# The tail of a one-token decode block: the folded sum kept in PSUM, two engines copying it out, and a store of four 512-byte rows

## The chip, the core and the metric

The kernel runs on one core of one Trainium2 chip. The core has five engines with their own instruction streams (TensorE or PE for matrix products, VectorE or DVE, ScalarE or ACT, GpSimd or POOL, SyncE or SP for issuing transfers), which meet only through semaphores, and 16 DMA engines that move data between HBM and the on-chip memory SBUF. TensorE writes its products to a second on-chip memory, PSUM (128 partitions, 8 banks of 512 fp32 numbers on each). The metric is the device time of one execution in microseconds; lower is better.

## The reference, cut to what matters

One token `x` of width 1024 goes through two branches, and the results are added to it.

```python
xn = layernorm(x)
# A: attention of 32 heads over the last W = 4096 places of a cache with 4 key/value heads
q = (xn @ wq)                                  # 1024 -> 32 heads x 128
p = softmax(q . k_cache[:, :, Sk - W:, :] * 128 ** -0.5)
A = (p . v_cache[:, :, Sk - W:, :]).reshape(4096) @ wo      # 4096 -> 1024
# B: a second layernorm and an MLP
B = gelu(layernorm(xn) @ w1 + b1) @ w2 + b2    # 1024 -> 3584 -> 1024
return x + A + B
```

Every weight and cache entry is used once. In bf16 wq, wo, the keys' window and the values' window and w1 and w2 come to some 39.9 MB that must be read from HBM; the output is 1024 bf16 numbers, 2 KB.

## The kernel before, in words

All big loads are issued by SP on one queue, in this order: wq in two pieces, the key window, w1, the value window; w2 once the product with wq is done (it takes over wq's place in SBUF); wo once the product with w1 is done (it takes over the places of w1 and of the keys). wo is laid out so that each of the 128 partitions holds 32 consecutive rows of it; "row j" below is the j-th row of every partition, a 128 x 1024 slab. Its 32 rows come in pieces of 16, 8, 4 and 3 rows (`WO_CHUNKS`), and row 31 comes as two loads, one for each half of its 1024 columns, with a semaphore each (lines 425 to 427).

TensorE multiplies a vector by such slabs with the array cut into four column groups of 32: a column of the vector, repeated 32 times, is the stationary operand, and the slab streams past. Four rows are worked on at a time, one in each group, so that partitions 0, 32, 64 and 96 of two PSUM banks (`SB` and `SB + 1`, banks 4 and 5, half the columns each) collect four partial sums. Both w2's 28 rows (`row_loop`) and wo's rows 0 to 27 (`four_rows`) add to them, and so do x and b2: lines 541 to 543 multiply a selection matrix `SELX` by `XB4`, which holds x's quarters on partitions 0, 32, 64, 96 and b2's on 1, 33, 65, 97.

Around the pieces of wo PE waits for transfers. After each of the first three pieces the kernel issues one fp32 product of no use (`keep_busy`, line 298; 512, 320 and 128 columns by `BUSY`), whose result nobody reads.

What follows row 27 is the tail:

- the copies: DVE copies bank 4 and ACT bank 5 to SBUF as `S` (lines 554 and 555)
- the fold: four fp32 matmuls of 256 columns (line 559) multiply a vector with ones at partitions 0, 32, 64, 96 by `S`. Column group a gets the a-th 128 columns of either half, into bank 0
- rows 28 to 31 (`fin_load`, `fin_half`): here all four column groups work on the same row, each on its own 128 columns of one half, so that nothing is left to be folded. The halves go to banks 7 and 6 (`HB`). Rows 28 to 30 wait for the piece of three rows; the first half of row 31 waits for its load, the second half for its own
- the end: DVE copies the fold from bank 0 to SBUF (`BULK`, line 578); then for each half it adds `BULK` and the bank into `ORow` as bf16 (line 582); SP waits for the second addition and issues the store of `ORow` (line 585), as eight runs of 256 bytes, two from each of four partitions; and SP waits for that store to land.

The small loop written behind the last matmul (lines 571 to 574) is a branch that PE takes once; the change doesn't touch it.

## Time and profile before

| | |
|---|---|
| three runs | 99.14, 99.17 and 99.19 us, median 99.17 |
| the profiled execution | 99.34 us, of which the span from the first to the last instruction is 98.0 |
| busy in the span | PE 53.2 us, PE's weight loads 13.4, DVE 41.8, ACT 11.2, POOL 8.2 |
| read from HBM | 39.86 MB, 407 GB/s over the span |
| queue of SP and ACT | 1740 packets, 95.0% of the 16 DMA engines' span |
| mean granted TensorE clock | 0.93 of full speed |
| the store's issue on SP (line 585) | 0.69 us, from 96.27 |

The times in the profile are microseconds from the first instruction of the span. A row of the timeline gives the start, the length, the engine and line, the operation with what it writes and reads, and how many instructions it merges; in square brackets is how long the engine had been idle and what released it. PEld stands for PE's weight loads, SPq and ACTq for the queues of DMA issues. A table by stretches gives for each stretch of time its length, then the busy time of each engine with the number of instructions, the granted PE clock, the share of the DMA engines and their rate.

### The profile page before, as it was taken

The numbers are of one execution on the slowest core, as the hardware profiler recorded it, in microseconds if no ns is written. First come the engines' busy times: TensorE is split into PE (matmuls) and PEld (weight loads), VectorE is DVE, ScalarE is ACT, GpSimd is POOL, SyncE is SP. The second block draws the span as 40 slices with busy tenths as digits, with TensorE's granted clock in tenths as the row PEclk, the third lists the DMA queues.
The fourth block names the chain that finished last, engine by engine and source line by source line (L and its number), as shares of the span: only waits on it lengthen the run. The fifth ranks groups of instructions, "written<-read, shape, count | busy, mean of one in ns | idle before, by whom it ended". The sixth has DMA issues, their size and how long they took to land.

```text
span 98.0 us, 911 instructions
## 1 busy us (share of the span) xinstructions
PE 53.2 (54%) x376; PEld 13.4 (14%) x217; DVE 41.8 (43%) x45; ACT 11.2 (11%) x21; POOL 8.2 (8%) x33
## 2 busy tenths in 40 slices
PE   0000232007960947195361489878998677883781
PEld 0000220001100001011010111113332111220130
DVE  0000321000028899999999500987943400110042
ACT  0000527000022000000000489000000000000020
POOL 6776201000000000000000000000000000000000
PEclk9999999999999589957999755899999999999999
DMA  3999888999999988899599998889994999999960
GB/s 53 488 613 398 377 374 375 398 538 441 428 428 578 398 374 374 374 398 702 237 428 428 428 588 374 374 374 398 702 398 214 428 428 428 421 428 408 421 251 1
DMA packets 1765, 39.87 MB, mean 407 GB/s; under 512 B 216, under 2 KB 484, under 8 KB 612
## 3 DMA queue, kind: packets, MB, share of 16 engines
q1 hardware_dynamic: 1740, 39.85, 95.0%
q10 hardware_dynamic: 24, 0.01, 0.0%
q14 instruction: 1, 0.01, 0.0%
HBM read 39.86 MB, written 0.00 MB: 407 GB/s over the span
## 4 chain that ended last, share of the span: by engine, by line
DMA 52%; DVE 24%; PE 11%; POOL 5%; issue 3%; SPq 1%; ACT 1%; POOLq 0%; DVEq 0%
DMA KT<-in_A_k_cache_dram 26%; DMA KT<-in_A_wo_dram 26%; DVE KT L355 18%; PE PS L292 9%; DVE MX L375 2%; DVE MX L377 2%; POOL F L206 1%; POOL B1R L188 1%; SPq L166 1%; DVE KT L554 1%; DVE MR L388 1%; PE PS L559 1%; ACT Q L381 1%; POOL QB L198 1%; PE PS L283 1%
## 5 line engine op out<-in xcount | busy, mean ns | idle before, releaser
L355 DVE STREAM_TRANSPOSE KT<-KT 128x4096 bf16<-128x4096 bf16 x4 | 17.4, 4413 | 0.5 <-DMA KT<-in_A_k_cache_dram 0.5
L283 PE MATMUL PS<-KT,QB 128*128 128x512 bf16 x32 | 8.9, 427 | 7.6 <-DVE KT L355 7.6
L283 PE MATMUL PS<-WA,XNTb 128*32 128x512 bf16 x64 | 6.8, 605 | 7.4 <-DMA WA<-in_A_wq_dram 7.4
L292 PE MATMUL PS<-W,YTb 128*32 x64 | 8.2, 464 | 1.3 <-issue 0.9
L292 PE MATMUL PS<-V,WA 128*128 (+1 forms) x31 | 7.9, 381 | 0.5 <-issue 0.2
L292 PE MATMUL PS<-WA,GT 128*32 x56 | 6.7, 381 | 2.6 <-issue 1.8
L253 PE MATMUL PS<-XT,onesf 128*128 128x16 f32 x2 | 0.6, 385 | 10.9 <-POOL XT L251 10.9
L327 DVE CAST Q<-PS 128x512 bf16<-128x512 f32 x1 | 0.7, 691 | 12.6 <-PE PS L283 12.6
L242 DVE STREAM_TRANSPOSE XT<-XB 128x256 bf16<-128x256 bf16 x1 | 0.6, 625 | 9.7 <-DMA XB<-in_A_x_dram 9.7
L406 DVE STREAM_TRANSPOSE WA<-WA 128x4096 bf16<-128x4096 bf16 x1 | 4.4, 4436 | 0.0
L292 PE MATMUL PS<-W,OT 128*32 128x512 bf16 x48 | 2.9, 380 | 2.1 <-DMA W<-in_A_wo_dram 1.5
L367 PEld LDWEIGHTS <-QB 128*128 128x128 bf16 x16 | 1.7, 104 | 17.3 <-DVE KT L355 13.5
L554 DVE COPY KT<-PS 128x512 f32<-128x512 f32 x1 | 0.7, 692 | 7.6 <-PE PS L292 7.6
L520 DVE TENSOR_TENSOR OD<-PS,D 128x128 f32<-128x128 f32 x1 | 0.3, 292 | 8.4 <-PE PS L518 8.4
L292 PEld LDWEIGHTS PS<-V,WA 128*128 (+1 forms) x32 | 3.1, 96 | 4.7 <-issue 3.0
L283 PE MATMUL PS<-MRow,ML 128*128 128x512 bf16 x8 | 3.3, 581 | 0.7 <-DVE QB L348 0.7
L402 ACT ACTIVATE WA<-PS,NMB 128x1024 bf16<-128x1024 f32 (+1 forms) x2 | 3.1, 1536 | 1.2 <-DVE NMB L397 1.2
L381 ACT ACTIVATE Q<-PS 128x512 f32<-128x512 f32 x1 | 0.6, 597 | 22.5 <-DVE MX L377 22.5
L555 ACT ACTIVATE KT<-PS 128x512 f32<-128x512 f32 x1 | 0.6, 597 | 22.2 <-PE PS L292 22.2
L312 PEld LDWEIGHTS <-XNTb 128*32 128x32 bf16 x32 | 1.2, 138 | 12.1 <-DMA WA<-in_A_wq_dram 8.3
L292 PEld LDWEIGHTS PS<-W,YTb 128*32 x32 | 1.6, 98 | 7.5 <-issue 7.1
L257 ACT ACT_TABLE_LOAD x1 | 1.3, 1283 | 10.9 <-POOL XT L251 10.9
(105 smaller groups left out, 47.4 us busy)
## 6 DMA issues: line engine op xcount, KB each, us to landing
WA<-in_A_wq_dram SPq DMA_DIRECT2D x1, 7168.0 KB, 21.5
W<-in_B_w_dram SPq DMA_DIRECT2D x1, 7168.0 KB, 42.2
WA<-in_B_w_dram SPq DMA_DIRECT2D x1, 7168.0 KB, 47.4
KT<-in_A_k_cache_dram SPq DMA_DIRECT2D x1, 4096.0 KB, 25.9
V<-in_A_v_cache_dram SPq DMA_DIRECT2D x1, 4096.0 KB, 51.3
W<-in_A_wo_dram SPq DMA_DIRECT2D x1, 4096.0 KB, 18.9
W<-in_A_wo_dram SPq DMA_DIRECT2D x1, 2048.0 KB, 23.4
WA<-in_A_wq_dram SPq DMA_DIRECT2D x1, 1024.0 KB, 5.0
```

Of the source, the lines that this page charges most:

```text
L257: C["std1"] = ACT.mark(act.activation(out=msx[:, 6:7], in_=msx[:, 5:6], func=ACTF.Sqrt, scale=-1.0, bias=EPSC[:, 0:1]))
L283: return pe.add_instruction(mybir.InstMatmult(name=nc.get_next_instruction_name(), engine=PEE, ldweights=load, start_tensor_calc=start, st ...
L292: return pe.add_instruction(mybir.InstMatmult(name=nc.get_next_instruction_name(), engine=PEE, ldweights=load, start_tensor_calc=start, st ...
L312: pe.ldweights(w, tile_position=(0, 32 * a))
L355: C["kt"].append(d(dve.transpose(KT[:, j * W:(j + 1) * W], KT[:, j * W:(j + 1) * W])))
L367: pe.ldweights(w, tile_position=(0, 0))
L375: d(dve.tensor_reduce(out=MX[:, 0:1], in_=PS[:, 0:2048], axis=AX.X, op=ALU.max))
L377: C["mx1"] = d(dve.tensor_reduce(out=MX[:, 1:2], in_=PS[:, 2048:4096], axis=AX.X, op=ALU.max))
L381: C["s7"] = ACT.mark(act.activation(out=S7, in_=bank(7), func=ACTF.Copy))
L402: C[f"exp{j}"] = C["exp"] = ACT.mark(act.activation(out=PT[:, lo:lo + n], in_=src, func=ACTF.Exp, bias=NMB[:, 0:1], scale=SCALE, accum_out ...
L406: C["PT"] = d(dve.transpose(PT, PT))
L554: C["S0"] = d(dve.tensor_copy(S[:, 0:DH2], bank(SB)))
```

## The change

- x and b2: one weight load of all of `SELX` and two matmuls of 128 columns on the whole array, which start banks 7 and 6 anew. They no longer go into banks 4 and 5.
- The fold is eight fp32 matmuls of 128 columns that add to banks 7 and 6 in place of four of 256 columns that start bank 0. Column group a now holds the a-th quarter of the output, its first 128 columns in bank 7 and the others in bank 6.
- Rows 28 to 31 add to the same places, and none of them starts a bank.
- The third `keep_busy` (128 columns, after row 27) is gone.
- Row 31 is one load with one semaphore, and both of its halves wait for that.
- The copy `BULK` and the two additions are gone: ACT copies bank 7 and DVE bank 6 into `ORow`, and SP waits for both. The store has four runs of 512 bytes.

```diff
-BUSY = (512, 320, 128)
+BUSY = (512, 320)
...
-    out_rows = out.rearrange("b s (h a n) -> (b s a) h n", h=2, a=4)
+    out_rows = out.rearrange("b s (a n) -> (b s a) n", a=4)
...
-    for h in range(2):
-        sp.dma_start(KT[:, 7 * D + h * DH2:7 * D + (h + 1) * DH2], wo_p[:, 31, h * DH2:(h + 1) * DH2]).then_inc(
-            s_wo[4 + h], 16)
+    sp.dma_start(KT[:, 7 * D:8 * D], wo_p[:, 31, :]).then_inc(s_wo[4], 16)
...
-    def fin_half(c, h, first, last):
+    def fin_half(c, h):
         for a in range(4):
-            lo = (c - WO_W1) * D + h * DH2 + a * DQ
-            ins = held(PS[32 * a:32 * a + 32, HB[h] * 512:HB[h] * 512 + DQ], KT[:, lo:lo + DQ],
-                       OT[:, c:c + 1].to_broadcast([128, 32]), (0, 32 * a), (128, 32), first, last)
+            lo = (c - WO_W1) * D + a * 2 * DQ + h * DQ
+            ins = go(quarter(a, h), low(KT[:, lo:lo + DQ], OT[:, c:c + 1].to_broadcast([128, 32])), (0, 32 * a), (128, 32),
+                     False, True, True, False)
         return ins
+    def quarter(a, h):
+        return PS[32 * a:32 * a + 32, HB[h] * 512:HB[h] * 512 + DQ]
...
-    for a in range(4):
-        pe.matmul(bank(SB + a // 2, (a % 2) * 256, 256)[32 * a:32 * a + 32, :], lhsT=SELX[:, 32 * a:32 * a + 32],
-                  rhs=XB4[:, :], start=False, stop=True, skip_group_check=True)
+    pe.ldweights(SELX[:, :], tile_position=(0, 0))
+    for h in range(2):
+        go(bank(HB[h], 0, DQ), low(XB4[:, h * DQ:(h + 1) * DQ], SELX[:, :]), (0, 0), (128, 128), True, True, True, False)
...
-        keep_busy(BUSY[j])
+        else:
+            keep_busy(BUSY[j])
...
-    for a in range(4):
-        last = pe.matmul(PS[32 * a:32 * a + 32, 0:2 * DQ], lhsT=I32[:, 0:1].to_broadcast([128, 32]),
-                         rhs=S[:, :].rearrange("p (h y) -> p h y", h=2)[:, :, a * DQ:(a + 1) * DQ], start=True, stop=True)
-    C["bulk"] = PE.mark(last)
+    for h in range(2):
+        for a in range(4):
+            pe.matmul(quarter(a, h), lhsT=I32[:, 0:1].to_broadcast([128, 32]),
+                      rhs=S[:, a * 2 * DQ + h * DQ:a * 2 * DQ + (h + 1) * DQ], start=False, stop=True, skip_group_check=True)
...
     fin_load(31)
+    pe.wait_ge(s_wo[4], 16)
     for h in range(2):
-        pe.wait_ge(s_wo[4 + h], 16)
-        C[f"fin{h}"] = PE.mark(fin_half(31, h, False, True))
+        C[f"fin{h}"] = PE.mark(fin_half(31, h))
...
-    dve.wait_ge(PE.sem, C["bulk"])
-    d(dve.tensor_copy(BULK[:, :], bank(0, 0, 2 * DQ)))
-    dw()
-    for h in range(2):
-        dve.wait_ge(PE.sem, C[f"fin{h}"])
-        C["out"] = d(dve.tensor_tensor(out=ORow[:, h * DQ:(h + 1) * DQ], in0=bank(HB[h], 0, DQ),
-                                       in1=BULK[:, h * DQ:(h + 1) * DQ], op=ALU.add))
-    sp.wait_ge(DVE.sem, C["out"])
-    sp.dma_start(out_rows, ORow[0:128:32, :].rearrange("p (h n) -> p h n", h=2)).then_inc(s_out, 16)
+    act.wait_ge(PE.sem, C["fin0"])
+    C["out0"] = ACT.mark(act.activation(out=ORow[:, 0:DQ], in_=bank(HB[0], 0, DQ), func=ACTF.Copy))
+    dve.wait_ge(PE.sem, C["fin1"])
+    C["out1"] = d(dve.tensor_copy(ORow[:, DQ:2 * DQ], bank(HB[1], 0, DQ)))
+    sp.wait_ge(ACT.sem, C["out0"])
+    sp.wait_ge(DVE.sem, C["out1"])
+    sp.dma_start(out_rows, ORow[0:128:32, :]).then_inc(s_out, 16)
     sp.wait_ge(s_out, 16)
```

More of the change, by code (lines that the diff above doesn't have):

```diff
@@ L80, in bass_parallel_sum__sliding_block_cached__mixer_channel_mlp__decode_kernel @@
     s_v = sems("s_v", 1)
-    s_wo = sems("s_wo", len(WO_CHUNKS) + 2)
+    s_wo = sems("s_wo", len(WO_CHUNKS) + 1)
     s_w2 = sems("s_w2", len(W2_CHUNKS))
@@ L142, in bass_parallel_sum__sliding_block_cached__mixer_channel_mlp__decode_kernel @@
     OT = sb("OT", [128, 32], bf16)
-    BULK = sb("BULK", [128, 256], f32)
     ZERO = sb("ZERO", [128, 1], bf16)
@@ L565, in bass_parallel_sum__sliding_block_cached__mixer_channel_mlp__decode_kernel @@
         for h in range(2):
-            fin_half(c, h, c == WO_BULK, False)
+            fin_half(c, h)
     fin_load(31)
+    pe.wait_ge(s_wo[4], 16)
     for h in range(2):
-        pe.wait_ge(s_wo[4 + h], 16)
-        C[f"fin{h}"] = PE.mark(fin_half(31, h, False, True))
+        C[f"fin{h}"] = PE.mark(fin_half(31, h))
     nc.br("once", engines=[PEE])
```

## The prediction

> **What bounds the kernel now.** I read the page first. Its slices of DMA use are at 8 or 9 nearly everywhere up to the third from the last; the kernel streams 39.86 MB at 407 GB/s over the span, and the last bytes of wo come at the end.

> ```profile
> DMA  3999888999999988899599998889994999999960
> ```

> Nothing in the change touches the stream before wo's last row, so I next read the chain of waits from there, cut to the tail, to see what is left after the last byte.

> ```profile
> 67.64 25.42 DMA KT<-in_A_wo_dram
> ...
> 94.51 0.64 PE PS L559 x8
> 95.15 0.50 PE PS L283 x28
> ...
> 95.75 0.50 DVE ORow L582 x2
> ```

> The chain goes through the copy (0.70, left out here) and the fold (line 559). Whether they really decide is seen from row 31's matmuls. Here is the table by stretches for line 283 alone (length, PE busy, number of instructions):

> ```profile
> 95.40:95.60 0.20, 0.20 (x20) 1.00 0.16 41
> 95.60:95.64 0.04, 0.03 (x4) 1.00 0.00 0
> 95.64:95.68 0.04, 0.00 (x0) 1.00 0.00 0
> 95.68:95.92 0.24, 0.22 (x4) 1.00 0.00 0
> ```

> All but four of the 32 matmuls of rows 28 to 31 are over at 95.64, then PE is empty, and the last four run alone from 95.69. So the end is set by the landing of row 31's second half, and copy and fold have time to spare. The transfers agree: the last packets in the stretch from 95.0 (40 slices of 10 ns) are those of one late DMA engine, one line of 1 KB every 42 ns.

> ```profile
> GB/s 0 102 0 0 0 102 0 0 0 0 102 0 0 0 102 0 0 0 0 0 0 0 0 0 0 0 0 0 0 0 0 0 0 0 0 0 0 0 0 0
> ```

> After that, the timeline and, for the store's packets, the transfers from 97.4 (40 slices of 10 ns again):

> ```profile
> 95.41 0.50 PE L283 MATMUL PS<-KT,OT 128*32 128x128 bf16 x8
> 95.75 0.50 DVE L582 TENSOR_TENSOR ORow<-PS,BULK 128x128 bf16<-128x128 f32 x2
> 96.27 0.69 SPq L585 DMA_DIRECT2D out_dram<-ORow  x1
> ...
> GB/s 0 0 0 0 0 0 0 0 0 0 0 0 0 0 0 0 26 26 51 52 0 26 0 26 0 0 0 0 0 0 0 0 0 0 0 0 0 0 0 0
> ```

> The two additions take 0.292 us each and overlap (0.50 together), so the second starts at 95.96, on the heels of the last matmul (95.69 + 0.24 = 95.93), and ends at 96.25. SP issues at 96.27 for 0.69 (96.96), the packets start 0.61 later (97.56 to 97.65), and the span ends at 98.02. The largest piece of this tail is the store: 1.75 us, of which 0.69 is its issue.

> **The change part by part**, against the profiled execution: 98.0 of span and 1.3 around it make 99.34, which is 0.17 above the median of 99.17. Differences are carried over to the median.

> 1. Row 31 as one load. A late engine has 8 lines of 2 KB to move in place of 16 of 1 KB. At the stream's 428 GB/s (26.8 per engine, the page's slices for wo) 1 KB would take 38 ns; it takes 42, so a line costs 4 ns of its own. Eight lines fewer are 0.035, the completion write of the other load about 0.01: landing 0.045 earlier. Ends: 0 (the lines overlap anyway) and 0.07 (twice the 4 ns). SP issues one load less (0.45 us, line 426), at 69 us, when nothing waits for SP.

> 2. Both halves of row 31 wait for it. Formerly the first half's four matmuls ran in the shadow of the second half's landing; now eight follow the landing. 20 matmuls in 0.20 us after 95.40 were mostly tails; the pace is that of 24 matmuls of rows 28 to 30 from 95.07 to 95.41, 0.34 us for six groups of four: 0.056 a group. So +0.055, and the last result is at 95.69 - 0.045 + 0.055 + 0.24 = 95.94.

> 3. The copies. `BULK`'s copy (0.42) lay beside the matmuls and its removal gives nothing. DVE's copy of 128 columns: copies of 512 and 256 columns took 0.692 and 0.425, so 128 take 0.292, as the addition did: 0. ACT's copy of bank 7 is not in the trace; the nearest row is 32x128 in 0.27 (line 350). It begins 0.055 before DVE's and is no longer, so it ends first: 0. If it cost as much as ACT's 512 columns (0.60) it would end 0.25 after DVE; that is an upper end I don't take, since 512 columns are four times the work.

> 4. SP waits twice. The wait for ACT is one more instruction, over before DVE's copy ends if ACT is first; the chain's row for such an instruction on DVE (line 581) is 0.02. I take +0.02; ends 0 and 0.05.

> 5. The store's issue, the term that matters. SP's rows for one-level patterns after an idle time (line 166: wq, w2, wo's first) are 0.383, 0.336 and 0.328; its only row for a two-level pattern after an idle time is the key window's, 0.642, and the store before is two-level too, at 0.687. After the change it is one-level, four lines.

> ```profile
> L173 SPq DMA_DIRECT2D KT<-in_A_k_cache_dram x1: 642/642/642, 6.4 to 6.4; - x1
> ...
> L166 SPq DMA_DIRECT2D W<-in_A_wo_dram x2: 328/380/433, 66.8 to 67.2; - x2
> ...
> L246 ACTq DMA_DIRECT2D XB<-in_B_b_dram x1: 503/503/503, 10.3 to 10.3; - x1
> ```

> The row of the same shape, four lines of 512 B, is ACT's load of b2: 0.503. So the gain is 0.18 by that row and 0.26 to 0.31 by SP's own (0.642 less 0.383 or 0.328). The queue that issues is SP, so I take its smallest, -0.26, with b2's 0.18 pulling the same way. Ends: 0 (it is the only store in the trace, and the length may be the store's own) and -0.36 (0.687 less 0.328). A loss is out: only the kernel's first load on ACT was longer than 0.687, and that was the first of its queue.

> 6. The store's data. The eight packets of 256 B, two on each of four engines, lie within 0.1 us; four of 512 B carry the same bytes. I take 0; ends 0 and -0.05 (half of the 0.1).

> [...]

> 7. The fold. Sixteen instructions of 128 columns in place of eight of 256, as much to stream. The old ones start in two groups (four in 94.47:94.75, the others to 95.06), 0.24 each, and all eight weight loads are over in the first. Expected 4 x 0.12, the same 0.48. Bounds: 0.48, and +0.42 if each of the four groups waits for a weight load of 0.106. Cover: rows 28 to 30 need 0.34 and row 31 can't start before 95.645, so the fold may last until 95.30, 0.31 later than now. At 0.42 it costs 0.11; I take 0.

> 8. x and b2. Four weight loads and four matmuls (0.29 us from 85.33) become one and two. PE waits for `OT` until 86.18 either way: 0.

> 9. The third `keep_busy` (0.49 us from 93.65) ran in the wait for DVE's copy, until 94.47: 0 if the clock holds.

> Sum: -0.045 + 0.055 + 0.02 - 0.26 = -0.23: 99.34 becomes 99.11, the median 98.94.

> **Rivals.**

> *The store's issue keeps its length.* Then -0.045 + 0.055 + 0.02 = +0.03: 99.20, no change. For it: no other store is in the trace. Against it: SP's one-level and two-level rows differ. At b2's 0.503 the sum is -0.15, 99.02, and that, too, counts as the same.

> *The 256-byte writes were slow to finish*, and wider ones aren't. The span ends 0.37 us after the store's last packet; that is the most that can go, and with half of it gone the sum is -0.23 - 0.18: 98.76. Against it: from the last packet of row 31 (95.19) to the matmul that waited for it (95.69) are 0.50, so small writes finish no later than large loads.

> *The clock falls without the third `keep_busy`* (slower). The table by stretches of 3.4 us, the length of the clock's steps here (length, PE busy, PE loads, DVE, ACT, POOL, clock, DMA):

> ```profile
> 38.27:41.69 3.42, 0.99 (x6) 0.19 (x2) 3.42 (x2) 0.00 (x0) 0.00 (x0) 1.00 0.66 285
> 41.69:45.10 3.41, 2.69 (x7) 0.30 (x2) 3.41 (x1) 0.00 (x0) 0.00 (x0) 0.50 1.24 538
> ...
> 89.47:92.89 3.42, 1.77 (x18) 0.50 (x10) 0.00 (x0) 0.00 (x0) 0.00 (x0) 1.00 0.99 412
> ...
> 91.60:95.01 3.41, 2.33 (x24) 0.85 (x16) 0.69 (x1) 0.60 (x1) 0.00 (x0) 1.00 0.92 364
> ```

> After the stretch with 0.99 us busy the next runs at 0.50; after the one with 1.77 the clock stays at 1.00. The stretch with the third `keep_busy` would go from 2.33 to 1.84, above 1.77. Should it fall all the same, fold (0.48), rows 28 to 30 (0.34) and row 31 (0.11) double; less the 0.31 of cover that is +0.62, with the store's gain +0.39: 99.55. [...]

> *The fold overruns* (slower): if all 16 weight loads of 0.106 stand in line with the matmuls it lasts 1.7 us longer, 1.4 beyond the cover: 100.3. Against the old 0.48 it is slower from 1.22 us on (0.48, 0.31 of cover, the 0.23 of gain, and 0.2). The eight loads of the old fold stood in nobody's way.

> **How the numbers follow.** Forecast, with the issue between 0.33 and 0.48 us: 52 in 100, -0.16 to -0.35, 98.82 to 99.00, nearly all of it faster. Issue longer than that: 24, from 99.0 to 99.22, the same. Slow small writes on top: 6, 98.6 to 98.8, faster. Clock: 5, 99.55. Fold or a wait behind it (ACT's copy at its upper end, +0.25): 13, 99.4 to 100.3, slower, less 1 that ends at the same. About 0.2% (0.2 us) is what a measurement here tells from no change. Moving some 7 of the forecast's 52 that give less than 0.2 us to the same: faster 0.51, same 0.30, slower 0.19. The range reaches from 98.75 to 99.40: it leaves out half of the slow small writes and most of the slower cases. The likeliest case's own is 98.82 to 99.00.

> **What would show it.** The issue on SP at 0.33 to 0.5 us in place of 0.69; eight matmuls of row 31 in one run of some 0.28 us behind one landing near 95.64; ACT's copy over before DVE's; SP's issue within 0.05 of 96.28; the sixteen fold instructions over by 95.3; the clock at 1.00 to the end. I am wrong if the issue stays near 0.69, if row 31's first matmul comes later than 95.7 because rows 28 to 30 are late, or if the clock shows 0.5 in the tail.

## The result

| | kernel before | changed kernel |
|---|---|---|
| median, 22 executions each | 99.19 us (99.09 to 99.49) | 99.83 us (99.10 to 100.27) |
| ratio | 1 | 1.0051, 95% interval 1.0031 to 1.0072 |
| the profiled execution | 99.34 us, span 98.0 | 100.17 us, span 97.9 |
| span, all executions of the changed kernel | | 97.8 to 98.1 us |
| total less span | 1.3 us in the profiled one | 1.27 to 1.36 us in ten executions, 1.92 to 2.37 us in twelve |

The change makes the kernel slower, where 98.94 was forecast, and the median lies outside the range (98.75 to 99.40). The last row of the table is needed to understand the number: the executions of the changed kernel fall into two groups, which have the same span and differ only in the time around it. Below, an execution with 1.6 us or more around its span is called one with a *late end*. Without the late ends the median of the changed kernel is 99.26, 0.07 above the kernel before.

There are then two results to explain: inside the span nothing was gained, where 0.23 us had been forecast, and outside it 0.6 to 1.1 us were lost in about half of the executions.

### The profile page after: what moved, and what is told of

It reads as the page before. It is cut to its first block, busy times and chain, and to the rows that moved or that the text cites. A ratio compares the mean times of both kernels' runs of the same rounds, so it can differ in the third digit from the quotient of the medians.

```text
span 97.9 us, 916 instructions
## 1 busy us (share of the span) xinstructions
PE 52.5 (54%) x380; PEld 13.1 (13%) x220; DVE 41.2 (42%) x43; ACT 11.4 (12%) x22; POOL 8.2 (8%) x33
## 3 DMA queue, kind: packets, MB, share of 16 engines
HBM read 39.86 MB, written 0.00 MB: 407 GB/s over the span
## 4 chain that ended last, share of the span: by engine, by line
DMA 54%; DVE 24%; PE 10%; POOL 5%; issue 3%; SPq 2%; ACT 1%; POOLq 0%
DMA KT<-in_A_wo_dram 28%; DMA KT<-in_A_k_cache_dram 26%; DVE KT L354 18%; PE PS L291 9%; DVE MX L374 2%; DVE MX L376 2%; SPq L165 2%; POOL F L205 1%; POOL B1R L187 1%; DVE MR L387 1%; ACT Q L380 1%; POOL QB L197 1%; POOL I L198 0%; POOL XB L186 0%; POOL identf L195 0%
## 6 DMA issues: line engine op xcount, KB each, us to landing
WA<-in_B_w_dram SPq DMA_DIRECT2D x1, 7168.0 KB, 47.4
```

## The profile after, inside the span

The page of the changed kernel: its span, and the use of the DMA engines in 40 slices.

```profile
span 97.9 us, 916 instructions
...
DMA  2998888999999988899699998888994999999960
```

The stream looks as before. Next, the tail from the timeline of the changed kernel (start, length, engine and line, operation, how many; in brackets the idle time before it and what ended that).

```profile
93.69 0.69 DVE L555 COPY KT<-PS 128x512 f32<-128x512 f32 x1 [7.63 <-PE PS L291]
94.44 0.38 PEld L561 LDWEIGHTS PS<-KT,I 128*32 128x32 f32 x16 [1.30 <-DVE KT L555]
94.44 0.64 PE L561 MATMUL PS<-KT,I 128*32 128x128 f32 x16 [0.79 <-DVE KT L555]
...
94.93 0.89 PE L291 MATMUL PS<-KT,OT 128*32 128x128 bf16 x32
95.81 0.28 ACT L579 ACTIVATE ORow<-PS 128x128 bf16<-128x128 f32 x1 [1.51 <-PE PS L291]
95.86 0.29 DVE L581 CAST ORow<-PS 128x128 bf16<-128x128 f32 x1 [1.48 <-PE PS L291]
96.25 0.66 SPq L584 DMA_DIRECT2D out_dram<-ORow  x1
```

Three things are to be seen. The 16 fold instructions have their weight loads behind them at 94.82 (94.44 + 0.38), and rows 28 to 30, whose piece lands at 94.89, start at 94.93: the fold does not overrun. The two copies take 0.28 and 0.29 us, and ScalarE's, which starts first, ends first (96.08 against 96.15). And the store's issue takes 0.66 us; the forecast had 0.43.

The table by stretches for the line that issues row 31's matmuls (length, PE busy and number of instructions, PE loads, clock, DMA share, GB/s):

```profile
95.50:95.54 0.04, 0.00 (x0) 0.00 (x0) 1.00 0.00 0
95.54:95.60 0.06, 0.06 (x6) 0.00 (x0) 1.00 0.00 0
95.60:95.66 0.06, 0.06 (x8) 0.00 (x0) 1.00 0.00 0
95.66:95.90 0.24, 0.16 (x8) 0.00 (x0) 1.00 0.00 0
```

PE is empty ahead of 95.54, since row 31's load lands at 95.50; then all eight matmuls of the row run behind that landing, the second half starting 0.055 us after the first. The clock is 1.00 in all of these stretches.

## The profile after, outside the span

The page ends with the span. The transfers of the changed kernel's profiled execution after it, from 98.5 to 100.6 (40 slices of 52.5 ns), are one packet:

```profile
DMA  0000000000000090000000000000000000000000
...
DMA packets 1, 0.02 MB, mean 8 GB/s; under 512 B 0, under 2 KB 0, under 8 KB 0
...
q8 instruction: 1, 0.02, 3.3%
```

It begins in the fifteenth slice, at 99.24 to 99.29, and takes 3.3% of sixteen engines' 2.1 us, which is 1.1 us of one engine. It is 16 KB that the profile calls "instruction"; I take it for a block of a program on its way into an engine. An 8 KB one on another queue (q14) is in the profile of nearly every kernel here; in this one it starts at 95.49 and takes 0.44 us, in the kernel before at 95.55 and 0.51, beside the tail. The one of 16 KB comes 1.3 us after the span's end and is over near 100.4. The profiled execution has a late end (2.27 us around the span, 100.17 in all).

Which engine's program? The packet's row doesn't say. On the page TensorE runs by far the most instructions (380 products and 220 weight loads, where VectorE has 43, GpSimd 33 and ScalarE 22), and the compiled program tells what the change did to its length: it grew from 435 to 442 instructions, 16 more for the fold, 5 fewer for x and b2, 4 fewer without the third `keep_busy`. That the block is TensorE's was thus an assumption at first; what speaks for it is `e11_before_pad12` below, where twelve weight loads more on TensorE and nothing else bring a packet of this size and queue into the stream. So the experiments began with the question whether TensorE's longer program, ScalarE's late copy, the wider rows of the store or the missing `keep_busy` made the late end.

## Experiments: which part makes the late end

In the expectations of the first runs the theories are these: the length of TensorE's program (A, where a letter stands for it), ScalarE's copy as one of the last instructions (B), the store's wider rows (C), the changed order of TensorE's last instructions (D) and the missing `keep_busy` (E).

**TensorE's program lengthened alone** (`e1_before_pad7`), the kernel before:

```diff
+    for _ in range(7):
+        pe.ldweights(ML[:, :], tile_position=(0, 0))
     pe.ldweights(ML[:, :], tile_position=(0, 0))
```

> The kernel before with seven more weight loads of the mask ML on PE (where PE waits for DVE's transposes anyway), so that PE's stream has 442 instructions as the changed kernel's has, in place of 435. In the changed kernel the span is 97.8 to 98.1 us in all 22 executions, but half of them take 1.3 us around it and half 2.0 to 2.3. Theory A (PE's stream has grown by seven instructions over a limit, and the end of the program is fetched late): some executions near 100.1, others near 99.2, spans near 98.0. Theory B (ACT now ends its program 1.8 us later) and theory C (the store's four wide rows, or SP's second wait): all executions within 99.1 to 99.5.

Measured: 99.2 us, ratio 1.0011 (1.000 to 1.0023); one execution of 11 had 1.65 us around its span, the others 1.30 to 1.35. The length 442 is not enough for what the change does.

**No ScalarE at the end** (`e2_after_dve_copies`), the changed kernel with both copies on VectorE and one wait on SyncE:

```diff
-    act.wait_ge(PE.sem, C["fin0"])
-    C["out0"] = ACT.mark(act.activation(out=ORow[:, 0:DQ], in_=bank(HB[0], 0, DQ), func=ACTF.Copy))
+    dve.wait_ge(PE.sem, C["fin0"])
+    d(dve.tensor_copy(ORow[:, 0:DQ], bank(HB[0], 0, DQ)))
...
-    sp.wait_ge(ACT.sem, C["out0"])
```

> The changed kernel with both final copies on DVE, so that ACT's last instruction is again the copy of S at 94 us, and SP waits once. PE's stream stays at 442 instructions. The span should be 0.2 longer (two copies of 0.29 that overlap a little), 98.1. Theory A: still two groups of times, 0.8 to 1.0 apart. Theory B, and SP's second wait: one group near 99.4. The store's rows: two groups.

**A late ScalarE copy in the kernel before** (`e3_before_act_late`), whose result nobody reads:

```diff
+    act.wait_ge(PE.sem, C["fin1"])
+    act.activation(out=LATE[:, :], in_=bank(SB, 0, DQ), func=ACTF.Copy)
```

> The kernel before with one copy by ACT of 128 columns of an idle bank behind the last matmul, into a scratch tile that nobody reads or waits for. PE's stream stays at 435 instructions. Theory A: one group near 99.2. Theory B: two groups, near 99.2 and 100.1.

Measured: without ScalarE at the end the changed kernel still has a late end in 4 of 12 executions (1.95 to 2.49), median 99.28, ratio 1.0044 (1.0017 to 1.0071). The kernel before with a late ScalarE copy has 99.2 us, ratio 1.0006 (0.9996 to 1.0017), and one execution of 11 at 1.64. So the late end doesn't need ScalarE at the end, and a late ScalarE copy alone doesn't bring it.

**The kernel before with one load for row 31 and a store of four 512-byte rows** (`e6_before_load_store`); the columns of fold and rows 28 to 31 are renumbered as in the change:

```diff
-    out_rows = out.rearrange("b s (h a n) -> (b s a) h n", h=2, a=4)
+    out_rows = out.rearrange("b s (a n) -> (b s a) n", a=4)
...
-        sp.dma_start(KT[:, 7 * D + h * DH2:7 * D + (h + 1) * DH2], ...
+    sp.dma_start(KT[:, 7 * D:8 * D], wo_p[:, 31, :]).then_inc(s_wo[4], 16)
...
-    sp.dma_start(out_rows, ORow[0:128:32, :].rearrange("p (h n) -> p h n", h=2)).then_inc(s_out, 16)
+    sp.dma_start(out_rows, ORow[0:128:32, :]).then_inc(s_out, 16)
```

> The kernel before with row 31 as one load and the store as four rows of 512 bytes (the columns of fold and rows 28 to 31 are mapped to suit), all else as it was: fold in bank 0, BULK, two additions, three keep_busy, 435 instructions on PE. Theory C: two groups of times, near 99.2 and 100.1. Theories D and E: one group. By the profile after, the span should be that of the kernel before within 0.1, since the store's issue took 0.66 us there, too.

Measured: 99.41 us in four executions, ratio 0.9992 (0.9936 to 1.0048; two of the seven executions of the kernel before beside it have a late end), 1.3 us around the span in all. That no late end shows in four executions says little of the rows of the store: if a third were late, four would be free of it once in five times. The issue of the store, here with one wait and with neither the new fold nor the new copies, takes 0.652 us:

```profile
L583 SPq DMA_DIRECT2D out_dram<-ORow x1: 652/652/652, 96.5 to 96.5; - x1
```

**No `keep_busy` at all** (`e4_after_no_busy`), to see whether the clock or its margin has a part:

```diff
-        else:
-            keep_busy(BUSY[j])
```

> The changed kernel without the two remaining keep_busy products, 434 instructions on PE. Theory A: one group, and if the clock holds near 99.1 (span 97.9, 1.2 to 1.3 around it). Theories B and C: still two groups. The stretches without these products have 1.0 us or less of PE work in 3.4 us, so the granted clock may fall to one half in the tail; then the rows from 94.4 on take twice as long and the span is up to 0.6 longer.

Measured: 100.19 us, ratio 1.0114 (1.0097 to 1.0131), but in the span (98.7 to 98.9); one late end in five. The table by stretches of the clock's steps, for this kernel and then for the changed one (length, busy time of PE, PE loads, DVE, ACT, POOL, clock, DMA share, GB/s):

```profile
89.01:92.42 3.41, 1.04 (x16) 0.20 (x8) 0.00 (x0) 0.00 (x0) 0.00 (x0) 1.00 0.95 398
92.42:95.83 3.41, 2.11 (x33) 0.99 (x28) 0.69 (x1) 0.60 (x1) 0.00 (x0) 0.50 0.65 263
```

```profile
92.77:96.18 3.41, 1.88 (x56) 0.85 (x36) 0.98 (x2) 0.88 (x2) 0.00 (x0) 1.00 0.58 232
89.36:92.77 3.41, 1.77 (x18) 0.50 (x10) 0.00 (x0) 0.00 (x0) 0.00 (x0) 1.00 0.95 395
```

After a stretch with 1.04 us of PE work the clock is at 0.50 and the tail longer by 1 us; after stretches with 1.77 and 1.88 it stays at 1.00. The first two `keep_busy` together are worth that microsecond, the third was not needed. The margin is small: in the last run below (`e18_after_pv3_swap`) a stretch with 1.61 us, from 93.17 to 96.58, is followed by 0.50. It costs nothing there, since TensorE's work is over, but in the stretches at the end of these traces 1.77 us of work held the clock and 1.61 didn't.

## Experiments: the length of TensorE's program

The next three undo or add single parts, and they showed something that none of the theories above had.

**The third `keep_busy` put back** (`e5_after_busy3`), 446 instructions:

```diff
-BUSY = (512, 320)
+BUSY = (512, 320, 128)
...
-        else:
-            keep_busy(BUSY[j])
+        keep_busy(BUSY[j])
```

> The changed kernel with the third keep_busy (128 columns) put back, 446 instructions on PE. Theory D (the changed order of PE's last instructions makes the end of its program late): two groups of times again, near 99.2 and 100.1, since PE's stream is no shorter. Theory E (the dropped product leaves PE cold or idle at the end, and that makes the end late): one group near 99.2. Theory C (the store's four wide rows): two groups.

**The kernel before with the fold in PSUM and two copies** (`e7_before_fold_in_psum`), 447 instructions; the third `keep_busy` is left out here, too, and rows 28 to 31 add to the fold, while x and b2, the two loads of row 31 and the two-level store stay as before:

```diff
-    for a in range(4):
-        last = pe.matmul(PS[32 * a:32 * a + 32, 0:2 * DQ], ...
+    for h in range(2):
+        for a in range(4):
+            pe.matmul(PS[32 * a:32 * a + 32, HB[h] * 512:HB[h] * 512 + DQ], lhsT=I32[:, 0:1].to_broadcast([128, 32]),
+                      rhs=S[:, h * DH2 + a * DQ:h * DH2 + (a + 1) * DQ], start=True, stop=True, skip_group_check=True)
...
+    C["out0"] = ACT.mark(act.activation(out=ORow[:, 0:DQ], in_=bank(HB[0], 0, DQ), func=ACTF.Copy))
+    C["out"] = d(dve.tensor_copy(ORow[:, DQ:2 * DQ], bank(HB[1], 0, DQ)))
```

> The kernel before with the fold as eight matmuls into banks 7 and 6, rows 28 to 31 adding to it, no third keep_busy, and the two results copied by ACT and DVE; x and b2, the two loads of row 31 and the store of eight runs stay as before. 447 instructions on PE. Theory D: two groups of times. Theory C: one group near 99.2. Theory E: two groups.

**The changed kernel with 24 weight loads more, early in the program** (`e8_after_pad24`), 466 instructions:

```diff
+    for _ in range(24):
+        pe.ldweights(ML[:, :], tile_position=(0, 0))
```

> The changed kernel with 24 more weight loads on PE early on, where it waits for DVE: 466 instructions. If the late end goes by where in PE's stream the last instructions lie, the share of late ends changes: none, or all. If it goes by the order or the timing of the last instructions themselves, or by the store, about half of the executions stay late.

Measured: 100.62, 100.56 and 100.56 us; ratios 1.0115 (1.0058 to 1.0172), 1.0108 and 1.0108 (1.0052 to 1.0164 both). None has a late end; all have spans of 99.1 to 99.5 us, 1.2 to 1.4 longer. In each, the 16 KB block is in the stream, at 73, 62 and 62 us. So the theory was formed anew: beyond a certain length TensorE's next block is fetched while the weights stream, on one of the 16 DMA engines, which then brings its share of w2 a microsecond late. That was tested on the kernel before, with nothing but the length changed.

**Twelve weight loads more** (`e11_before_pad12`), 447 instructions; the edit is that of the seven with `range(12)`:

> The kernel before with twelve weight loads more on TensorE ahead of its first score matmuls, 447 instructions and nothing else changed. Length theory: the next block of TensorE's instructions is now fetched within the span, at some 60 to 73 us, one DMA engine is held for a microsecond, w2 lands about 1.2 us later and the span is 99.1 to 99.3 us with 1.3 us around it: median 100.5 us, ratio 1.013. If it is what the added instructions do at the end (the fold in PSUM, two copies) and not their number: 99.2 us as with seven loads more.

Measured: 100.44 us, ratio 1.0112 (1.0083 to 1.014), span 98.9 to 99.4, 1.28 to 1.36 us around it in all 12. The transfers of this kernel from 70.5 to 72.5 (40 slices of 50 ns), its load of w2 (KB, us from issue to landing), the same load in the kernel before, and the first matmuls with w2 on the timeline:

```profile
GB/s 0 0 1147 3441 2294 2294 1147 1147 4588 328 1147 0 0 0 0 0 0 0 0 0 0 0 0 0 0 0 0 1147 0 0 0 0 0 0 0 0 0 0 0 0
...
q8 instruction: 1, 0.02, 2.9%
```

```profile
WA<-in_B_w_dram SPq DMA_DIRECT2D x1, 7168.0 KB, 50.0
```

```profile
WA<-in_B_w_dram SPq DMA_DIRECT2D x1, 7168.0 KB, 47.4
```

```profile
77.54 0.65 PE L292 MATMUL PS<-WA,GT 128*32 x4 [2.33 <-DMA WA<-in_B_w_dram]
```

In the first fence the packets start at 70.6 to 71.05 on the 16 engines, the one of 16 KB among them (the slice with 328 GB/s, 70.95; 2.9% of 16 engines' 2 us is 0.93 us), and one engine starts its next data packet only at 71.85 (the lone 1147). Fifteen engines land w2 at 75.25 to 75.58 us (in the kernel before all sixteen at 75.45 to 75.97), one at 77.06; PE waits 2.33 us for it. In the kernel before w2 takes 47.4 us from issue to landing, here 50.0. The one engine stays behind, since it has its share of wo to bring too: row 31's last part lands at 96.76 against 95.65. That is the 1.1 us of the span.

**The kernel before without its branch hint** (`e16_before_no_hint`), 430 instructions. The kernel marks a place ahead of the product with wq and gives it as a hint to the branch behind PE's last matmul; mark and branch go:

```diff
-    hinted = pe.mark_branch_hint_location()
...
-    nc.br("once", engines=[PEE])
-    with nc.body("once", valid_engines=[PEE]):
-        pe.br_lt(pe.zero_reg, 0, on_true="once", on_false="on").branch_hint(hinted)
-    nc.switch_bb("on")
```

> The kernel before without the branch hint that is set ahead of the first product and without the branch that it belongs to, 430 instructions in TensorE's program. If the hint is what brings the last block of TensorE's instructions in before the end, the block is now fetched late: 1.9 to 2.4 us around the span in all or most executions, median 99.9 to 100.2 us, or the fetch falls into the span and the span is longer by up to 1.2 us. If the block comes in ahead of need by itself, 99.2 us as before, or a little less by the branch's own time on TensorE, which lies beside the last copies.

Measured: 100.41 us, ratio 1.0103 (1.007 to 1.0136), span 98.9 to 99.3. The transfers from 62 to 64, and w2:

```profile
GB/s 0 0 0 0 2294 0 2294 0 3441 8028 328 0 1147 0 0 0 0 0 0 0 0 0 0 0 0 0 0 0 1147 0 0 0 0 0 0 0 0 0 0 0
...
q8 instruction: 1, 0.02, 2.9%
```

```profile
WA<-in_B_w_dram SPq DMA_DIRECT2D x1, 7168.0 KB, 48.9
```

The block is fetched at 62.5, in the stream, though the program is shorter than before. So the hint (with its branch, which went too) and the short program together are what keeps this fetch out of the weights' way in the kernel before, for 1.2 us. With 442 instructions the changed kernel is still inside that, by at most three instructions: 446 are too many.

## Experiments: is the late end a matter of length too?

With 442 instructions the block is not in the stream, and the late ends have to be explained apart. The theory was that the same fetch, put off to the end, comes too late by a little; a shorter program should cure it.

**The changed kernel, three products with V to a turn in place of five** (`e9_after_pv3`), 436 instructions: `PV_UNROLL = 3`.

> The change with one constant altered: the loop of 30 products with V is written out three to a turn instead of five, so TensorE's program is 436 instructions long instead of 442, one more than before the change; the same matmuls run in the same order. Length theory (the last block of TensorE's instructions is fetched late, after the span, because the program has grown): time around the span 1.3 us in nearly all executions, median 99.2 us, ratio 1.000 within 0.002, and a block fetched on TensorE's queue, if one shows, before 97 us. Order theory (it is the new last matmuls and the two copies that delay the closing code, whatever the length): about half the executions with 1.9 to 2.4 us around the span, as with 442 instructions, median near 99.8 us. If the ten shorter turns cost time themselves, the span grows and the loop's rows show it; I expect nothing, since TensorE waits for w2 behind that loop.

**The same with two products to a turn, and SyncE's waits swapped** (`e10_after_pv2_swap`), 433 instructions:

```diff
-PV_UNROLL = 5
+PV_UNROLL = 2
...
-    sp.wait_ge(ACT.sem, C["out0"])
     sp.wait_ge(DVE.sem, C["out1"])
+    sp.wait_ge(ACT.sem, C["out0"])
```

> The change with two repairs: two products with V to a turn (433 instructions in TensorE's program) and SyncE's two waits in the other order (VectorE's first, ScalarE's second). Length theory: no late ends, time around the span 1.3 us. If the wait that is given last becomes an instruction of its own and the one given first sits on the store, as the profile after the change suggests, the store is issued some 0.06 us earlier after VectorE's copy than there (0.091 us after the copy's end): span 97.8 to 97.9, median 99.10 to 99.15 us, ratio 0.999. If the order of the waits does not matter: 99.2 us. Order theory as for the run before: half the executions around 100 us.

**The kernel before with three products to a turn** (`e12_before_pv3`), 429 instructions:

> The kernel before with three products with V to a turn: 429 instructions in TensorE's program instead of 435. Length theory: no late end in any execution; median as before, 99.15 to 99.2 us, ratio 1.000 within 0.001. Should it be clearly faster than the kernel before, a block of instructions cost that one something too that its trace does not show.

Measured: the first has 99.21 us, ratio 0.9991 (0.9952 to 1.0029), late ends in 2 of 12. The second has no late end, but spans of 97.8 to 99.4 and 99.63 us; without its four longest executions (spans of 99.3 and 99.4) the ratio is 0.9996 (0.9956 to 1.0036). The profiled one is among the four, and in it the loop's turns are too short: PE is idle ahead of the matmuls with V for 3.3 us, in 14 places, where the changed kernel has 0.2 us in one. The matmuls with V (count, ns least, median and most, first and last start), in the changed kernel and in this one:

```profile
L291 PE MATMUL PS<-V,WA x31: 379/379/389, 66.8 to 74.6; 128*128 x30, 128*128 128x512 bf16 x1
```

```profile
L291 PE MATMUL PS<-V,WA x32: 376/384/390, 67.6 to 80.3; 128*128 x30, 128*128 128x512 bf16 x2
```

With two to a turn they last until 80.3, beyond w2's landing at 75.66. My own expectation had looked only at whether a block of instructions was late. The third has 99.06 us, ratio 0.9961 (0.9927 to 0.9995), and one late end of 12 at 2.34. Without the late ends it has 99.04 against 99.21 us: three products to a turn alone make the kernel before a little faster; why is not shown. On this chip the kernel before itself had four late ends of 35 (2.19 to 2.49).

Since chips differ in this, the changed kernel was run again beside its variants.

**The changed kernel once more** (`e13_after_again`):

> The changed kernel itself once more, so that it stands beside the next three on one chip. Length theory and order theory alike: span 97.9 us, and 1.9 to 2.4 us around it in a third to two thirds of the executions (12 of 22 so far); median between 99.3 and 99.9 us.

**The changed kernel, wo's first sixteen rows in a loop** (`e14_after_short`), 418 instructions, with the waits swapped:

```diff
+        if j == 0:
+            row_loop(W1, OT, n, lambda v, u, i: v[:, bass.ds(i * 4 + u, 1)])
-        for c in range(sum(WO_CHUNKS[:j]), sum(WO_CHUNKS[:j + 1]), 4):
+        for c in range(sum(WO_CHUNKS[:j]) if j else n, sum(WO_CHUNKS[:j + 1]), 4):
```

> The change with the first sixteen rows of wo taken in a loop of four turns, as the rows of w2 are, in place of written-out instructions: TensorE's program is 418 instructions instead of 442, its last instructions are the same; SyncE's two waits are in the other order as in the next run. The loop's turns have slack, since the second piece of wo lands 2.5 us after the first. Length theory: no late end (0 or 1 of 12), 1.3 us around the span in the rest, median 99.10 to 99.25 us, ratio 0.998 to 1.001. Order theory: late ends as often as in the run of the change itself beside it, median 99.3 to 99.9 us.

**The changed kernel with SyncE's waits swapped** (`e15_after_swap`), 442 instructions; the edit is the second half of `e10_after_pv2_swap`'s:

> The change with SyncE's two waits in the other order: VectorE's first, ScalarE's second; 442 instructions as in the change. If the wait given first sits on the store and the one given last is an instruction of its own, the store is issued 0.05 to 0.06 us earlier after VectorE's copy, and executions without a late end are that much shorter than those of the change beside it; if not, they are equal within 0.03 us. Late ends as often as in the change itself, a third to two thirds, by both theories.

Measured: the changed kernel 99.22 us, ratio 1.0007 (0.9969 to 1.0046), late ends in 3 of 12 (2.40 to 2.48). The shortest program 100.2 us, ratio 1.0085 (1.0053 to 1.0117), because its loop is slower than the written-out rows (first row 86.47, last turn from 90.67, where the rows of the changed kernel take 1.9 us from 86.12) and the tail starts 1.3 us later; it has a late end in one of 7. That one was profiled; its transfers after the span (98.9), from 99 to 101.2 in slices of 55 ns, and, to compare, those of the changed kernel's execution without a late end (`e13_after_again`, total 99.32), from 96.5 to 98.5 in slices of 50 ns:

```profile
DMA  0000000000000000000090000000000000000000
...
q8 instruction: 1, 0.02, 3.1%
```

```profile
DMA  0000000000900000000001000000000000000000
...
q8 instruction: 1, 0.02, 3.7%
```

In the first the block comes at 100.10 to 100.16, 1.3 us after the span; in the second at 97.0, beside the store, and it is over (3.7% of 16 engines' 2 us: 1.2 us) at 98.2. Over all the profiles: both profiled executions with a late end fetch the block 1.3 us after the span; of those without a late end and without the block in the stream seven show it at 96.5 to 97.1 and six show none (a record can be missing: of the 32 matmuls with V the changed kernel's profile has 31), and none shows it after the span. The extra time in the two (0.8 and 1.0 us) is of the packet's size (1.1 us).

The traces show two things more. TensorE's branch behind its last product has a row; in the changed kernel's first profile, with the late end, it stands at 95.5 (95.55):

```profile
L575 PEldq COMPARE_BRANCH  x1: 82/82/82, 95.5 to 95.5; - x1
```

In the seven profiles without a late end that show the block near the end, it comes 1.0 to 1.7 us after this branch; in the two with a late end 3.7 and 4.0 us after it. And the kernel before with the fold in PSUM (`e7_before_fold_in_psum`) has two such packets, one in the stream at 62.4 and one at 98.8, 1.1 us after its branch:

```profile
q8 instruction: 2, 0.03, 0.1%
```

So the block in the stream and the block at the end need not be one fetch that is put off, as the theory had it.

The waits swapped: 99.33 us, ratio 1.0007 (0.9984 to 1.003), 4 late ends of 12 (1.89 to 2.01). The timeline of its tail:

```profile
95.66 0.28 ACT L579 ACTIVATE ORow<-PS 128x128 bf16<-128x128 f32 x1 [1.53 <-PE PS L291]
95.71 0.29 DVE L581 CAST ORow<-PS 128x128 bf16<-128x128 f32 x1 [1.50 <-PE PS L291]
96.03 0.66 SPq L584 DMA_DIRECT2D out_dram<-ORow  x1
```

VectorE's copy ends at 96.006 and the issue starts at 96.034, 0.028 later, where it took 0.091 in the changed kernel (96.154 to 96.245) and 0.027 in the kernel before (96.247 to 96.274). The wait that is given second does become an instruction of its own (17 ns), and if it is the one that ends last, it puts 0.064 us into the path.

**Seven weight loads where the change adds its instructions** (`e17_before_endpad7`), 442 instructions, the kernel before:

```diff
+    for _ in range(7):
+        pe.ldweights(SELX[:, :], tile_position=(0, 0))
     pe.wait_ge(s_wo[len(WO_CHUNKS) - 1], 16)
```

> The kernel before with seven weight loads more on TensorE, put behind the fold instead of early in the program: 442 instructions. If 442 instructions, the added ones at the end, are enough for the late end: 1.9 to 2.5 us around the span in a third to a half of 12 executions, median above 99.3 us. If it takes the change's own last instructions: 1.3 us around the span in all but 0 or 1, median 99.2 us, ratio 1.000 within 0.002.

**The changed kernel with 436 instructions and swapped waits** (`e18_after_pv3_swap`):

> The change with three products with V to a turn (436 instructions) and SyncE's two waits in the other order. If the shorter program makes the late end rare, at most 2 of 12 executions have it; the rest have spans of 97.7 to 97.9 us and the median is 99.08 to 99.18 us, ratio 0.998 to 1.000: no loss, and at most 0.1 us gained. If length below 446 does not matter: a third to a half late, median above 99.3 us.

Measured: the seven loads give 99.5 us, ratio 1.0031 (1.0019 to 1.0042), no late end in 6. The loss is in the span (98.1 to 98.3), and the timeline of its tail has it:

```profile
94.80 0.34 PEld L563 LDWEIGHTS <-SELX 128*128 128x128 bf16 x7 [0.41 <-issue]
...
95.14 0.40 PEld L531 LDWEIGHTS <-OT 128*32 128x32 bf16 x16
95.15 0.62 PE L283 MATMUL PS<-KT,OT 128*32 128x128 bf16 x32 [0.28 <-issue]
```

They take 0.34 us behind the fold; rows 28 to 30, landed at 94.71, start at 95.15, and all 32 matmuls follow one another to the end. From row 31's landing (95.38) to the store's issue (96.35) are 0.96 us, where the kernel before has 0.63 (95.65 to 96.27). The last run has 99.13 us, ratio 1.0014 (0.9991 to 1.0037), 3 late ends of 12; its other nine executions have a median of 99.08 against 99.18 of the kernel before beside them. It is the best version of the change, and no proven gain; three products to a turn had done as much for the kernel before (`e12_before_pv3`).

**All late ends together** (executions with 1.6 us or more around the span, programs without the block in the stream):

| kernels | instructions | late ends |
|---|---|---|
| the kernel before, all measurements | 435 | 7 of 134 |
| before, seven weight loads more (early, late) | 442 | 1 of 17 |
| before, late ScalarE copy; load and store; three products to a turn | 429 and 435 | 2 of 27 |
| changed kernel and variants (both measurements, VectorE alone, swapped waits) | 442 | 23 of 58 |
| variants of the change, shorter | 418 to 436 | 7 of 48 |

By these sums 442 instructions do not make the late end by themselves: 1 of 17 against 23 of 58 would come by chance about once in 160 draws, and without the first measurement, which raised the question, 1 of 17 against 11 of 36, once in 23. Programs shorter than the changed kernel's have fewer late ends, but not none: 5 of 24 with 436 instructions, 2 of 24 with 434 or fewer. The sums mix chips, and chips differ. Side by side, the changed kernel and its variants have 5 of 17 late ends where the kernel before has 0 of 29, 8 of 31 where it has 1 of 23, 3 of 12 where it has 0 of 18, but 2 of 24 where it has 4 of 35. So the end's own instructions seem to count, and the length perhaps too; neither is proved.

**What stays open** is which instructions: the fold in PSUM with sixteen instructions more, the product of x and b2, the missing third `keep_busy` and the store's wide rows are in all these variants, and the two runs that would have told them apart (the third `keep_busy` put back, the fold with the old x and b2 and the old store) went past 442 instructions and so met the other cost. Open, too, is what makes the fetch come later in one execution than in the next. That the late fetch *causes* the late end was not tried by taking the fetch away; it rests on the two profiles and the matching size, and one cause behind both is not ruled out. Counted from the span's first instruction, the two packets end at 100.41 and 101.25, each 0.24 us later than the measured times, 100.17 and 101.01, would end; how the measured time lies on the span's clock is not known, so it isn't shown that the time waits for the packet's end.

## Why the prediction was wrong, by its steps

Its sum went against 99.34, of which 1.3 us lie around the span, and it took these 1.3 for given. That unspoken step failed in half of the executions, and it is the larger part of the miss: 0.6 us in the median. In its place stand 1.92 to 2.37 us around the span in twelve of 22 executions; a block of instructions that is fetched late goes with them, and the cause stays open. Not one of the terms asked what seven more instructions or another order of them cost apart from their running time; x and b2 "0" and the fold "0" were right for the engines' time only.

Inside the span, by the two profiles:

| step | forecast | measured |
|---|---|---|
| 1 row 31 as one load: from the landing of rows 28 to 30 to row 31's | -0.045 | -0.01 (0.63 before, 0.62 after) |
| 2 both halves behind it: from the first matmul of what was waited for to the last copy's start | +0.055 | +0.057 (0.322 after 0.265) |
| 3 the copies | 0 | 0 (0.291 after 0.292) |
| 4 SyncE's second wait | +0.02 | +0.064 |
| 5 the store's issue | -0.26 | -0.03 (0.657 after 0.687) |
| 6 the store's data, from the issue's end to the span's | 0 | -0.015 (1.047 after 1.062) |
| sum | -0.23 | +0.06 |

The span itself is 0.07 shorter after than before (97.95 against 98.02), because rows 28 to 30 land 0.13 earlier in that execution (94.89 against 95.02), ahead of all that the change touches in the tail. It is from that landing to the end that the table counts: 3.06 us against 3.00.

- **Step 5 is the one that failed.** The reason given, that SyncE's loads with one level take 0.33 to 0.38 us and with two levels 0.64, does not carry over to a store: the store takes 0.65 to 0.66 in every kernel here with one level and 0.68 to 0.69 in every one with two. The end of 0 that the step named ("the length may be the store's own") was the right one. ScalarE's load of b2 (0.503), a row of the same shape, was a warning that the forecast took for support of the same sign.
- **Step 4** had its bound (0.05) a little low. It had ScalarE's wait over first and so out of the way; but the compiled program puts the later-given wait, VectorE's, on an instruction of its own, so that this instruction's 17 ns and the way from it to the store stand behind the last copy. The swapped order shows both.
- **Step 1** gave 0.014 of its 0.045 in these two profiles. Over the others without a block in the stream, the distance between the two landings is 0.64 to 0.68 us with two loads and 0.60 to 0.64 with one, so a gain of a few hundredths is likely, and its size is not shown.
- **Step 2** was right in size: 0.055 us a group, in the table of stretches above.
- **Steps 7, 8 and 9** held. The fold took its 0.48 us and did not overrun; the clock stayed at 1.00 with 1.91 us of PE work from 91.60 to 95.01, where 1.84 had been worked out. That stretch does not lie on the clock's own steps, though (they are at 89.36, 92.77 and 96.18 in the changed kernel's profile), so the forecast leaned on a stretch that is none of the clock's; the steps from 89.36 and 92.77 have 1.77 and 1.88. The run without any `keep_busy` shows the other side (1.04 us, then 0.50).
- **Step 6** held, and the rival of slow small writes did not come true: the time from the issue's end to the span's differs by 0.015 us (1.047 with rows of 512 bytes, 1.062 with rows of 256), where that rival had 0.18.
- **A sign that came true by luck**: the store's issue was to start within 0.05 us of 96.28, and it starts at 96.25. It does so because the stream landed 0.13 earlier; from row 31's landing to the issue are 0.745 us, where the forecast's own terms make 0.70 (0.626 before, and 0.055 and 0.02).
- **The chances** don't add up as told: by the parts given, "the same" has 24 + 7 + 1 = 32 in 100 and "slower" 5 + 12 = 17, where 0.30 and 0.19 stand. It changes nothing in the argument.

So the first rival came true inside the span: the store's issue keeps its length, forecast +0.03, measured +0.06, and the medians without late ends agree (+0.07 in the first measurement, 99.17 against 99.25 or -0.08 beside `e13_after_again`: no change that can be told). None of the rivals had the late end.

What a block of 16 KB goes with was measured: in the stream it cost 1.1 to 1.4 us of span in five kernels, and after the end it goes with 0.8 and 1.0 us in the two executions profiled.

## What to carry to other kernels

Count the instructions that an edit adds to an engine's program, not only their time. In this kernel, whose DMA engines are busy to the end (95.0% of the span), one block of 16 KB of code in the stream held one of them for a microsecond (0.93 to 1.02 us), and that engine's late share of w2 and wo set the end; the hint with its branch, or four instructions more (446 after 442), decided whether a block fell there. When the total moves and the span doesn't, look at the transfers outside the span before looking for a cause inside. And a duration is carried over from a row of the same direction and queue: the shape of a store's pattern did not give it the issue time of a load with that shape (0.65 to 0.66 us, where SyncE's one-level loads after an idle time had 0.33 to 0.38).
